# Exchanging transposed attention blocks through a scratch tensor in memory, in two halves of four heads, and letting early transposes share five PSUM banks with the mix

## The chip, the core and the metric

The kernel runs on one core of a Trainium2 chip. The metric is the device time of one execution in microseconds (us); lower is better. The core has a matrix engine (TensorE, PE in the rows; its weight loads are PEld), a vector engine (VectorE, DVE), a scalar engine (ScalarE, ACT), GpSimd (POOL) and a queue that issues transfers (SyncE, SP). Each of them runs its own instructions strictly in the order in which they are written, and waits where an instruction's inputs are not ready. Results of TensorE land in PSUM, which has eight banks of 128 x 512 float32 here; all else is held in SBUF.

## What is computed

Banded attention for 4 batches, 8 heads, 768 positions and head size 64: a position sees the first 8 keys and its last 96. Then a channel mix over the 512 channels (8 heads x 64).

```python
scores = scale * q @ k.T - slope[h] * dist          # masked outside of the band
a = softmax(scores)
x = (a @ v), heads side by side                     # [4, 768, 512]
x_prev = x moved by one position
xk = mu_k * x + (1 - mu_k) * x_prev
xr = mu_r * x + (1 - mu_r) * x_prev
kk = relu(xk @ w_k) ** 2                            # 512 -> 1024
out = sigmoid(xr @ w_r) * (kk @ w_v)                # 1024 -> 512
```

## The kernel before

The rows are cut into 24 tiles of 128 positions, six to a batch. For tile n and a pair of heads hp (0 to 3), `scores` multiplies queries with the keys of this tile and the one before (into a bank of `ps_s`), VectorE adds the bias and takes the maximum (L317), ScalarE takes the exponential (L318), and after every second pair GpSimd divides by the sums (L328). The weights of the softmax then lie with the query on the partition and must be turned, so that the key is on the partition, before `weighted` can multiply them with the values (L383, the matmuls named `av`).

Tiles 0 to 8 are turned by TensorE (`transposes`, L362) into banks of `ps_t`, and ScalarE copies them out (L363). From tile 9 on (`MOVED`), `turn` (L339, L341) has VectorE turn blocks of 32 x 32 in place into the area `turned`, and `exchange` (L349) then moves the blocks between groups of 32 partitions: 16 transfers for each tile, each from 32 partitions of `turned` to 32 partitions of `landed`, 64 KB (32 KB where the tile is the first of its batch). `turned` and `landed` each exist once.

The channel mix works on chunks of two tiles. For a chunk, `mix` makes xk and xr as pairs of a high and a low part; then TensorE makes `kp` (four banks one after the other), `z` (two) and `vps` (two), each product as three matmuls (L423 to L425), all in banks of one pool, `ps_f`. VectorE squares `kp` into `kk` (L466) and frees its bank. The first chunk works in plain float32 (L432, L453, L489), because the weights come as 64-bit words that are decoded meanwhile (`weight_begin`: L162 loads, L170 to L175 decode with three VectorE steps).

Tiles are worked in steps. In step n+1, `scores` of tile n+1 runs beside the turning of tile n; in step n+2, `weighted` of tile n is written first. Between the pairs of heads stand pieces of the mix of an earlier chunk. The order in which the program is written is not yet the order of the engines: a scheduler reorders the instructions of every engine, by its own estimate of when each is ready. So a change of a transfer or a pool can move instructions anywhere.

In the loop, the lines that matter are these:

```python
if hp == 0 and step > 1:
    for i in range(4):
        weighted(step - 2, i)
    global_v(step - 1)
if step:
    if hp < 2:
        turn(step - 1, 2 + hp)
    if hp == 1:
        exchange(step - 1)
    transposes(step - 1, hp)
```

Of the kernel before, what the change touches and what calls it, by code (L numbers as in the profile page):

```python
# [9 lines left out]
F32 = mybir.dt.float32  # L10
# [7 lines left out]
PSUM = bass.MemoryType.PSUM  # L18
# [3 lines left out]
NT = S // 128  # L22
# [3 lines left out]
MOVED = 9  # L26
# [7 lines left out]
def tile_biased_attention_channel_mix(ctx: ExitStack, tc: tile.TileContext, qT, kT, v, n_sizes, mu_kr, w_k, w_v, w_r, q_rows, k_rows, v_rows, slopes, out):  # L34
    nc = tc.nc
# [30 lines left out]
    fast = ExitStack()  # L66
    p4k = fast.enter_context(tc.tile_pool(name="p4k", bufs=3))
    kw_pool = fast.enter_context(tc.tile_pool(name="kw", bufs=2))
    q_pool = fast.enter_context(tc.tile_pool(name="qp", bufs=2))
    v_pool = fast.enter_context(tc.tile_pool(name="vp", bufs=3))  # L70
    r_pool = fast.enter_context(tc.tile_pool(name="rp", bufs=1))
    s_pool = fast.enter_context(tc.tile_pool(name="sp", bufs=3))
    x_pool = fast.enter_context(tc.tile_pool(name="xp", bufs=1))
    f_pool = fast.enter_context(tc.tile_pool(name="fp", bufs=1))
    f2_pool = fast.enter_context(tc.tile_pool(name="f2", bufs=4))
    ps_s = fast.enter_context(tc.tile_pool(name="ps_s", bufs=2, space=PSUM))
    ps_t = fast.enter_context(tc.tile_pool(name="ps_t", bufs=2, space=PSUM))
    ps_a = fast.enter_context(tc.tile_pool(name="ps_a", bufs=1, space=PSUM))
    ps_f = fast.enter_context(tc.tile_pool(name="ps_f", bufs=3, space=PSUM))


    zeros = const.tile([128, 256], BF16, name="zeros")
# [20 lines left out]
    j = flts[:, 224:352]  # L103
# [15 lines left out]
    for h in range(H):  # L119
        c = -8.0 * 2.0 ** -(h + 1)  # L120
# [14 lines left out]
    for h in range(H):  # L135
        c = -8.0 * 2.0 ** -(h + 1)
# [54 lines left out]
    def weights_go(begun):  # L191
        while w_count[0] < min(begun, len(w_steps)):
            weight_begin(w_count[0])
            w_count[0] += 1
# [6 lines left out]
    def pool_copy(dst, src):  # L201
        pool.tensor_scalar(dst, src, 1.0, 1.0, op0=ALU.mult, op1=ALU.mult)


    state = {}
    room = r_pool.tile([128, 12, 512], F32, name="room")
    turned = room[:, 4:8].rearrange("p b x -> p (b x)")
    landed = room[:, 0:4].rearrange("p a x -> p (a x)")
# [13 lines left out]
    def load_tile(n):  # L222
        b, t = divmod(n, NT)
        s = state[n] = {}
        if n < NATIVE:
            qr, kr = padded[n % 2], ring[:, n % 4]
            for o, h in sides:
                nc.sync.dma_start(qr[o : o + 64, h : h + HH], qT[n, :, h : h + HH])
                nc.sync.dma_start(kr[o : o + 64], kT[n, :, h : h + HH])
            s["qr"], s["kr"] = qr, kr  # L230
            return
        qr = p4k.tile([128, H, 128], F32, tag="t4k", name=f"qraw_{n}")
        if n == NATIVE:
            kr = kw_pool.tile([128, H, 256], F32, tag="kw", name=f"kraw_{n}")
        else:
            kr = p4k.tile([128, H, 128], F32, tag="t4k", name=f"kraw_{n}")
        for o in (0, 64):
            nc.sync.dma_start(qr[o : o + 64], qT[n])
        for o in (0, 64):
            if n == NATIVE:  # L240
                nc.sync.dma_start(kr[o : o + 64, :, 128:256], kT[n])
                if t == 1:
                    nc.sync.dma_start(kr[o : o + 64, :, 0:128], kT[n - 1])
                elif t:
                    nc.sync.dma_start(kr[o : o + 64, :, 0:32], kT[n - t, :, :, 0:32])
                    nc.sync.dma_start(kr[o : o + 64, :, 32:128], kT[n - 1, :, :, 32:128])
            else:
                nc.sync.dma_start(kr[o : o + 64], kT[n])
        s["qr"], s["kr"] = qr, kr

    def load_v(n):
        b, t = divmod(n, NT)
        va = v_pool.tile([128, DM], F32, name=f"va_{n}", tag="va")
        nc.sync.dma_start(va, v[b, t * 128 : (t + 1) * 128, :])
        state[n]["va"] = va

    def global_v(n):

        b, t = divmod(n, NT)
        if t >= 2:  # L260
            nc.sync.dma_start(state[n - 1]["va"][0:32], v[b, 0:32, :])
# [68 lines left out]
    def turn(n, hp):  # L330
        if n < MOVED:
            return
        s = state[n]
        w = 256 if n % NT else 128
        hk = w // 16
        src = room[:, 8 + hp].rearrange("p (u k) -> p u k", u=2)[:, :, 0:w]
        dst = turned[:, : 4 * hk * 32].rearrange("p (b g i) -> p g b i", b=4, g=hk)[:, hp * hk // 4 : (hp + 1) * hk // 4]
        if w == 256:
            vec.transpose(dst, src.rearrange("p u (g b j) -> p (u g) b j", b=4, j=32))  # L339
        else:  # L340
            vec.transpose(dst, src.rearrange("p u (b j) -> p u b j", b=4))  # L341

    def exchange(n):
        if n < MOVED:
            return
        m = 512 if n % NT else 256
        for b in range(4):
            for a in range(4):
                nc.sync.dma_start(landed[32 * b : 32 * b + 32, a * m : (a + 1) * m], turned[32 * a : 32 * a + 32, b * m : (b + 1) * m])  # L349

    def transposes(n, hp):
        if n >= MOVED:
            return
        s = state[n]
        nb = 2 if n % NT else 1
        pt = ps_t.tile([128, 512], F32, name=f"t_{n}_{hp}", tag="t")
        et = room[:, (4 * n + hp) % 5 if n < MOVED - 1 else hp]
        for u in range(2):
            e = s["e"].pop(2 * hp + u)
            for k in range(nb):  # L360
                c = (u * nb + k) * 128
                pe.transpose(pt[:, c : c + 128], e[:, k * 128 : (k + 1) * 128], ident)  # L362
        act.copy(et[:, : 2 * nb * 128], pt[:, : 2 * nb * 128])  # L363
        s["et", hp] = et

    def weighted(n, hp):
        t = n % NT
        s = state[n]
        if hp == 0:
            s["av"] = ps_a.tile([128, 512], F32, name=f"av_{n}", tag="av")  # L370
        blocks = [state[n - 1]["va"], s["va"]] if t else [s["va"]]
        nb = len(blocks)
        if n < MOVED:
            et = s.pop(("et", hp))
        else:
            et = landed[:, : 1024 * nb].rearrange("p (a g i) -> p g a i", a=4, i=32)
        for u in range(2):
            h = 2 * hp + u
            o = s["av"][64 * u : 64 * u + 64, hp * 128 : (hp + 1) * 128]
            for k, vt in enumerate(blocks):  # L380
                c = (u * nb + k) * 128
                g = et[:, c : c + 128] if n < MOVED else et[:, h * nb + k]
                pe.matmul(o, vt[:, h * 64 : (h + 1) * 64], g, start=k == 0, stop=k == nb - 1)  # L383
        if hp == 3:
            c, i = divmod(n, 2)
            if i == 0:
                if t == 0:
                    pool.memset(xt[:, :, 0:1], 0.0)
                else:
                    pool_copy(xt[:, :, 0:1], xt[:, :, 256:257])  # L390
            act.copy(xt[:, :, 1 + 128 * i : 129 + 128 * i], s["av"].rearrange("p (a q) -> p a q", a=4))  # L391
# [110 lines left out]
    def ffn(c):  # L502
        if c:
            xk, xr = (mix(xt[:, :, 1:257], xt[:, :, 0:256], tag, p4k, f_pool) for tag in "kr")
        else:
            xk, xr = (plain_mix(xt[:, :, 1:257], xt[:, :, 0:256], tag) for tag in "kr")
        return channel_mix(xk, xr, lambda i: out[(2 * c + i) * 128 : (2 * c + i + 1) * 128, :], f_pool, f2_pool, ps_f, c == 0, c == NCHUNK - 1)
# [20 lines left out]
    for step in range(NTILES + 1):  # L528
        if step + 1 < NTILES:
            load_tile(step + 1)  # L530
        if step < NTILES:
            load_v(step)
        for hp in range(4):
# [5 lines that stand above are left out]
                if hp < 2:  # L539
                    turn(step - 1, 2 + hp)  # L540
                if hp == 1:
                    exchange(step - 1)
                transposes(step - 1, hp)
            if step < NTILES:
                if hp > 1:
                    turn(step, hp - 2)
                scores(step, hp)
            if hp == 0:
                if step >= LAG and (step - LAG) % 2 == 0:
                    queue.append(ffn((step - LAG) // 2))  # L550
                    if len(queue) == 1 and step == LAG:
                        budget[0] = -17.5
            run_ffn(2.5)
            run_ffn(2.5)
            if hp == 1 and step + 1 < NTILES:
                split_tile(step + 1)
            slot = 4 * step + hp
            n = min(8, 2 + slot * 4 // 3) if slot < 6 else 8 + (slot - 5) * 6 // 7
            weights_go(n)
    for i in range(4):  # L560
        weighted(NTILES - 1, i)
# [171 lines left out]
```

## Time and profile before

| | |
|---|---|
| median of 3 runs | 499.7 us (495.23 to 500.42) |
| the profiled execution | 493.66 us, its span 491.9 us |
| busy in the span | PE 472.3 us (96%), DVE 372.2 us, ACT 279.9 us, POOL 261.9 us |
| granted TensorE clock | 0.999 of full speed |
| transfers | 61.55 MB, mean 125 GB/s |

The span runs from the first instruction to the last. [...] In a row of a timeline, a bracket such as [0.94 <-DMA room<-room] says how long the engine sat idle ahead of it and what ended that. `room` is the tile in which `turned` and `landed` lie, so `room<-room` is a transfer of the exchange.

### The profile page before, as it was taken

To read this page: it belongs to the slowest core of one execution; us is meant where nothing else is said; L and a number is where in the kernel's file an instruction comes from. 1 tells how busy PE (TensorE), PEld (TensorE's weight loads), DVE (VectorE), ACT (ScalarE), POOL (GpSimd) and SP (SyncE) were. 2 spreads that over 40 slices of the span, in tenths; PEclk is the share of its full clock that TensorE was granted. 3 is DMA by queue.
4 is the path that set the end of the run, shared out by engine and by line. 5 is a ranking of instruction groups with operands and counts; after the bars stand their busy time and mean duration, and the time that the engine had idled before them with its cause. 6 is when DMAs were issued, how large, how long until landed. Compare 5 with 4: busy or idle time off the path is not lost.

```text
span 491.9 us, 9755 instructions
## 1 busy us (share of the span) xinstructions
PE 472.3 (96%) x3300; PEld 404.8 (82%) x3300; DVE 372.2 (76%) x921; ACT 279.9 (57%) x654; POOL 261.9 (53%) x392
## 2 busy tenths in 40 slices
PE   8889989999999999999999999999999899999995
PEld 6568754697898898898898898898898798898985
DVE  6998978887977977877977778876977966952621
ACT  6796548254758656448558438638558448542320
POOL 6868448718657634834756724835756823703000
PEclk9999999999999999999999999999999999999999
DMA  6994690521432452483383484385364462330001
GB/s 208 304 293 136 212 229 8 130 69 45 122 93 71 107 141 69 125 210 93 112 191 95 112 211 123 103 212 127 96 169 126 125 167 65 102 97 29 26 2 49
DMA packets 32201, 61.55 MB, mean 125 GB/s; under 512 B 7056, under 2 KB 10384, under 8 KB 32144
## 3 DMA queue, kind: packets, MB, share of 16 engines
q1 hardware_dynamic: 32000, 60.85, 46.8%
q8 instruction: 28, 0.46, 0.4%
q14 instruction: 29, 0.24, 0.2%
q10 hardware_dynamic: 144, 0.00, 0.0%
HBM read 39.85 MB, written 6.29 MB: 94 GB/s over the span
## 4 chain that ended last, share of the span: by engine, by line
PE 44%; DVE 17%; DMA 11%; POOL 9%; ACT 7%; issue 5%; SPq 5%; POOLq 0%; DVEq 0%; ACTq 0%
PE vps L423 5%; PE vps L424 5%; PE vps L425 5%; POOL room L328 4%; PE kp L423 4%; PE av L383 4%; PE kp L425 4%; PE kp L424 4%; DMA kraw<-in_kT_dram 4%; DMA w<-in_w_v_dram 4%; ACT room L318 3%; SPq L349 3%; DVE room L317 3%; PE z L423 3%; PE z L424 3%
## 5 line engine op out<-in xcount | busy, mean ns | idle before, releaser
L328 POOL TENSOR_SCALAR room<-room,r 128x256 f32<-128x256 f32 (+1 forms) x192 | 122.5, 655 | 96.7 <-DVE r L325 51.6
L318 ACT ACTIVATE room<-room,nmax 128x256 f32<-128x256 f32 (+1 forms) x192 | 92.7, 485 | 73.1 <-DVE nmax L317 71.2
L423 PE MATMUL kp<-xk_hi,wk_hi 128*128 128x256 f32 x352 | 99.2, 283 | 0.0
L425 PE MATMUL kp<-xk_hi,wk_lo 128*128 128x256 f32 x352 | 98.7, 281 | 0.0
L424 PE MATMUL kp<-xk_lo,wk_hi 128*128 128x256 f32 x352 | 98.6, 280 | 0.0
L423 PE MATMUL vps<-wv_hi,kk_hi 128*128 128x512 f32 (+1 forms) x184 | 71.2, 387 | 0.0
L424 PE MATMUL vps<-wv_lo,kk_hi 128*128 128x512 f32 (+1 forms) x184 | 71.2, 387 | 0.0
L425 PE MATMUL vps<-wv_hi,kk_lo 128*128 128x512 f32 (+1 forms) x184 | 70.7, 384 | 0.0
L317 DVE CUSTOM_DVE_ANT_0 room<-s,pat 128x256 f32<-128x256 f32 (+1 forms) x192 | 68.2, 391 | 3.0 <-PE s L309 1.2
L423 PEld LDWEIGHTS kp<-xk_hi,wk_hi 128*128 128x128 f32 x352 | 66.7, 190 | 1.4 <-issue 0.8
L424 PEld LDWEIGHTS kp<-xk_lo,wk_hi 128*128 128x128 f32 x352 | 66.0, 187 | 1.0 <-issue 0.3
L425 PEld LDWEIGHTS kp<-xk_hi,wk_lo 128*128 128x128 f32 x352 | 66.0, 188 | 0.3 <-issue 0.3
L383 PE MATMUL av<-room,va 128*64 128x128 f32 x704 | 48.6, 279 | 6.0 <-DMA room<-room 2.5
L383 PEld LDWEIGHTS av<-room,va 128*64 128x64 f32 x704 | 39.5, 136 | 15.3 <-issue 9.1
L467 ACT CAST kk_hi<-kk 128x512 fp32r<-128x512 f32 x44 | 27.1, 617 | 34.0 <-DVE kk L466 34.0
L468 DVE TENSOR_TENSOR kk_lo<-kk,kk_hi 128x512 fp32r<-128x512 f32 x44 | 35.1, 797 | 15.0 <-ACT kk_hi L467 14.3
L339 DVE STREAM_TRANSPOSE room<-room 128x512 f32<-128x512 f32 x52 | 34.6, 693 | 10.7 <-POOL room L328 10.4
L400 POOL TENSOR_SCALAR mix_k<-x,mus 128x256 f32<-128x256 f32 x44 | 26.3, 616 | 28.2 <-ACT x L391 28.2
L425 PEld LDWEIGHTS vps<-wv_hi,kk_lo 128*128 128x128 f32 x184 | 34.6, 188 | 7.5 <-issue 0.2
L423 PEld LDWEIGHTS vps<-wv_hi,kk_hi 128*128 128x128 f32 x184 | 34.6, 188 | 6.8 <-issue 0.7
L424 PEld LDWEIGHTS vps<-wv_lo,kk_hi 128*128 128x128 f32 x184 | 34.5, 188 | 6.3 <-issue 0.5
L466 DVE TENSOR_TENSOR kk<-kp,kk 128x512 f32<-128x512 f32 x44 | 30.1, 683 | 10.7 <-ACT kk L460 10.5
(116 smaller groups left out, 1006.9 us busy)
## 6 DMA issues: line engine op xcount, KB each, us to landing
room<-room SPq DMA_DIRECT2D x208, 64.0 KB, 2.0
kraw<-in_kT_dram SPq DMA_DIRECT2D x36, 256.0 KB, 4.1
qraw<-in_qT_dram SPq DMA_DIRECT2D x34, 256.0 KB, 4.0
va<-in_v_dram SPq DMA_DIRECT2D x24, 256.0 KB, 3.4
out_dram<-sig SPq DMA_DIRECT2D x23, 256.0 KB, 2.2
w<-in_w_k_dram SPq DMA_DIRECT2D x8, 512.0 KB, 7.4
w<-in_w_v_dram SPq DMA_DIRECT2D x8, 512.0 KB, 6.2
w<-in_w_r_dram SPq DMA_DIRECT2D x4, 512.0 KB, 7.9
```

Of the source, the lines that this page charges most:

```text
L317: vec.tensor_tensor_reduce(out=e[:, :w], in0=o, in1=p[:, h, :], op0=ALU.add, op1=ALU.min, scale=-0.125, scalar=3.0e38, accum_out=s["nmax"] ...
L318: act.activation(e[:, :w], e[:, :w], AF.Exp, bias=s["nmax"][:, h : h + 1], scale=-1.0, accum_out=s["sum"][:, h : h + 1])
L328: pool.tensor_scalar(e[:, :w], e[:, :w], r[:, u : u + 1], 1.0, op0=ALU.mult, op1=ALU.mult)
L339: vec.transpose(dst, src.rearrange("p u (g b j) -> p (u g) b j", b=4, j=32))
L383: pe.matmul(o, vt[:, h * 64 : (h + 1) * 64], g, start=k == 0, stop=k == nb - 1)
L400: pool.tensor_scalar(tmp[:, j, :], xp[:, j, :], m1[:, j : j + 1], 1.0, op0=ALU.mult, op1=ALU.mult)
L423: pe.matmul(o, sh, mh, start=first, stop=False)
L424: pe.matmul(o, sh, ml, start=False, stop=False)
L425: pe.matmul(o, sl, mh, start=False, stop=last)
L466: vec.tensor_mul(kk, pv, kk)
L467: act.copy(kkh[:, 2 * fp : 2 * fp + 2, :], kk)
L468: vec.tensor_sub(kkl[:, 2 * fp : 2 * fp + 2, :], kk, kkh[:, 2 * fp : 2 * fp + 2, :])
```

## The change

The exchange of a tile is made in two halves, of heads 0 to 3 and of heads 4 to 7. Each half is first written as one transfer to a scratch tensor in memory (`moved`, two buffers), and then read back in four transfers, each of which fetches for 32 partitions its four blocks. The first half's exchange is written at hp 0 of the step, the second half's at hp 1. `turned` and `landed` are laid out so that each half is one piece. The pool `ps_t` with its two banks goes, and `ps_f` has five banks instead of three; the transposes of tiles 0 to 8 take theirs there.

```diff
+    d_pool = fast.enter_context(tc.tile_pool(name="dp", bufs=2, space=bass.MemoryType.DRAM))
...
-    ps_t = fast.enter_context(tc.tile_pool(name="ps_t", bufs=2, space=PSUM))
     ps_a = fast.enter_context(tc.tile_pool(name="ps_a", bufs=1, space=PSUM))
-    ps_f = fast.enter_context(tc.tile_pool(name="ps_f", bufs=3, space=PSUM))
+    ps_f = fast.enter_context(tc.tile_pool(name="ps_f", bufs=5, space=PSUM))
...
-        hk = w // 16
+        hk = w // 32
...
-        dst = turned[:, : 4 * hk * 32].rearrange("p (b g i) -> p g b i", b=4, g=hk)[:, hp * hk // 4 : (hp + 1) * hk // 4]
+        dst = turned[:, 1024 * (hp // 2) : 1024 * (hp // 2) + 128 * hk].rearrange("p (b g i) -> p g b i", b=4, g=hk)[:, hp % 2 * hk // 2 : (hp % 2 + 1) * hk // 2]
...
-    def exchange(n):
+    def exchange(n, half):
         if n < MOVED:
             return
-        m = 512 if n % NT else 256
+        m = 256 if n % NT else 128
+        s = state[n]
+        moved = d_pool.tile([128, 4 * m], F32, name=f"moved_{n}_{half}", tag="moved")
+        nc.sync.dma_start(moved, turned[:, 1024 * half : 1024 * half + 4 * m])
+        blocks = moved.rearrange("(a j) (b x) -> b j a x", a=4, b=4)
         for b in range(4):
-            for a in range(4):
-                nc.sync.dma_start(landed[32 * b : 32 * b + 32, a * m : (a + 1) * m], turned[32 * a : 32 * a + 32, b * m : (b + 1) * m])
+            nc.sync.dma_start(landed[32 * b : 32 * b + 32, 1024 * half : 1024 * half + 4 * m].rearrange("j (a x) -> j a x", a=4), blocks[b])
...
-        pt = ps_t.tile([128, 512], F32, name=f"t_{n}_{hp}", tag="t")
+        pt = ps_f.tile([128, 512], F32, name=f"t_{n}_{hp}", tag="f")
...
                 if hp == 1:
-                    exchange(step - 1)
+                    exchange(step - 1, 1)
+                if hp == 0:
+                    exchange(step - 1, 0)
```

The scheduler's order moves at three places. On TensorE, at tile 14: `av_14` are the matmuls of `weighted` for tile 14, `kp` those of the mix, `s_16_0` the first scores of tile 16. Before:

```order
L423 MATMUL kp_3308<-xk_hi_3147,wk_hi_66 128x256
L424 MATMUL kp_3308<-xk_lo_3148,wk_hi_66 128x256
L425 MATMUL kp_3308<-xk_hi_3147,wk_lo_2_783 128x256
L423 MATMUL kp_3376<-xk_hi_3147,wk_hi_66 128x256
L383 MATMUL av_14_3329<-room_194,va_13_2676 64x128
L383 MATMUL av_14_3329<-room_194,va_14_2887 64x128
```

After, from the last of `av_14` on:

```order
L386 MATMUL av_14_3304<-room_193,va_13_2663 64x128
L386 MATMUL av_14_3304<-room_193,va_14_2870 64x128
L308 MATMUL s_16_0_3331<-kw_16_3218,qh_16_3216 128x256
L309 MATMUL s_16_0_3331<-kw_16_3218,ql_16_3217 128x256
L308 MATMUL s_16_0_3331<-kw_16_3218,qh_16_3216 128x256
L309 MATMUL s_16_0_3331<-kw_16_3218,ql_16_3217 128x256
L426 MATMUL kp_3283<-xk_hi_3132,wk_hi_66 128x256
```

`av_14` has moved ahead of 17 matmuls with 256 columns: the four of `s_16_0` and 13 of `kp`, which stood before it.

On the transfer queue, the same tile: `qraw`, `kraw` and `va` are loads of queries, keys and values for later tiles, and the 16 transfers `room<-room` are the exchange of tile 14. Before:

```order
L248 DMA kraw_16_3110<-in_kT_dram 64x1024 x2
L254 DMA va_15_3115<-in_v_dram 128x512
L261 DMA va_13_2676<-in_v_dram 32x512
L349 DMA room_194<-room_194 32x512 x16
L497 DMA out_0_dram<-sig_3101 128x512
L238 DMA qraw_17_3321<-in_qT_dram 64x1024
```

After (`moved_14_0` and `moved_14_1` are the two halves):

```order
L349 DMA moved_14_0_3116<-room_193 128x1024
L352 DMA room_193<-moved_14_0_3116 32x4x256 x3
L254 DMA va_15_3094<-in_v_dram 128x512
L261 DMA va_13_2663<-in_v_dram 32x512
L352 DMA room_193<-moved_14_0_3116 32x4x256
L238 DMA qraw_17_3296<-in_qT_dram 64x1024
L349 DMA moved_14_1_3177<-room_193 128x1024
L238 DMA qraw_17_3296<-in_qT_dram 64x1024
L352 DMA room_193<-moved_14_1_3177 32x4x256 x4
L248 DMA kraw_17_3297<-in_kT_dram 64x1024 x2
```

The first half now stands ahead of the loads of values, which wait for `av_13`; behind the second turning only one write and four reads are left.

On the same queue in the first 100 us: `w64_14` to `w64_19` are loads of the weights w_v, `kraw_7` the keys of tile 7, `va_3` (32 rows) a slice that `av_4` needs, `va_5` values of tile 5. Before:

```order
L162 DMA w64_16_735<-in_w_v_dram 128x1024
L228 DMA qz_0_196<-in_qT_dram 64x512
L241 DMA kraw_7_1098<-in_kT_dram 64x8x128
L254 DMA va_5_895<-in_v_dram 128x512
L162 DMA w64_17_793<-in_w_v_dram 128x1024
L261 DMA va_3_534<-in_v_dram 32x512
L243 DMA kraw_7_1098<-in_kT_dram 64x8x128
L241 DMA kraw_7_1098<-in_kT_dram 64x8x128
L243 DMA kraw_7_1098<-in_kT_dram 64x8x128
L162 DMA w64_18_836<-in_w_v_dram 128x1024
L162 DMA w64_19_883<-in_w_v_dram 128x1024
```

After:

```order
L241 DMA kraw_7_1097<-in_kT_dram 64x8x128
L243 DMA kraw_7_1097<-in_kT_dram 64x8x128
L162 DMA w64_14_634<-in_w_v_dram 128x1024
L162 DMA w64_15_671<-in_w_v_dram 128x1024
L162 DMA w64_16_734<-in_w_v_dram 128x1024
L162 DMA w64_17_792<-in_w_v_dram 128x1024
L162 DMA w64_18_835<-in_w_v_dram 128x1024
L162 DMA w64_19_882<-in_w_v_dram 128x1024
L254 DMA va_5_894<-in_v_dram 128x512
L261 DMA va_3_533<-in_v_dram 32x512
```

All four loads of `kraw_7` now stand ahead of `w64_14`, and the slice of `va_3` behind `w64_19`. On TensorE `av_4`, of which two matmuls stood ahead of the matmuls on `z` before, now stands as a whole behind the last `vps` of the first chunk and the first `kp` of the second.

## Rows read from the trace of the kernel before

**Rows 1.** The page: the span, and TensorE's busy time.

```profile
span 491.9 us, 9755 instructions
PE 472.3 (96%) x3300; PEld 404.8 (82%) x3300; DVE 372.2 (76%) x921; ACT 279.9 (57%) x654; POOL 261.9 (53%) x392
```

**Rows 2.** TensorE's waits up to 100 us, then from 100 us on: us, times, longest.

```profile
PE av L383 <- DMA va<-in_v_dram: 2.4, 1, 2.4
PE t L362 <- POOL room L328: 2.4, 5, 0.8
...
PE av L383 <- DMA room<-room: 2.5, 2, 1.5
PE z L423 <- DVE kk L466: 1.4, 3, 0.5
```

**Rows 3.** Stretches of 20 us: busy PE, PEld, DVE, ACT, POOL; clock, DMA share, GB/s.

```profile
280.00:300.00 20.00, 18.56 (x151) 17.10 (x150) 14.39 (x33) 8.31 (x22) 7.29 (x11) 1.00 0.74 176
...
380.00:400.00 20.00, 18.49 (x145) 16.81 (x144) 15.39 (x38) 7.84 (x21) 13.01 (x20) 1.00 0.62 159
```

**Rows 4.** Timeline of TensorE at tiles 14, 15 and 20: start, us, instruction.

```profile
279.41 0.28 PE L423 MATMUL kp<-xk_hi,wk_hi 128*128 128x256 f32 x1
...
280.82 0.28 PE L423 MATMUL kp<-xk_hi,wk_hi 128*128 128x256 f32 x1
282.03 1.99 PE L383 MATMUL av<-room,va 128*64 128x128 f32 x32 [0.94 <-DMA room<-room]
...
301.32 0.39 PE L423 MATMUL vps<-wv_hi,kk_hi 128*128 128x512 f32 x1
301.55 0.39 PE L424 MATMUL vps<-wv_lo,kk_hi 128*128 128x512 f32 x1
301.87 2.02 PE L383 MATMUL av<-room,va 128*64 128x128 f32 x32
...
391.92 0.84 PE L383 MATMUL av<-room,va 128*64 128x128 f32 x11 [1.51 <-DMA room<-room]
```

**Rows 5.** Timeline of the transfer queue: exchanges of tiles 14, 15 and 20.

```profile
269.45 10.88 SPq L349 DMA_DIRECT2D room<-room  x16
...
286.90 13.04 SPq L349 DMA_DIRECT2D room<-room  x16
...
379.19 11.02 SPq L349 DMA_DIRECT2D room<-room  x16
```

**Rows 6.** Timeline of VectorE: the last turning of tile 14.

```profile
268.71 0.71 DVE L339 STREAM_TRANSPOSE room<-room 128x512 f32<-128x512 f32 x1 [0.20 <-POOL room L328]
```

**Rows 7.** Chain that ended last, by time: the last transfer of tile 12's exchange.

```profile
238.54 1.79 DMA room<-room
```

**Rows 8.** Transfers issued from 140 to 480 us: KB each, median us to landing.

```profile
room<-room SPq DMA_DIRECT2D x208, 64.0 KB, 2.0
...
out_dram<-sig SPq DMA_DIRECT2D x18, 256.0 KB, 2.2
va<-in_v_dram SPq DMA_DIRECT2D x15, 256.0 KB, 2.8
...
va<-in_v_dram SPq DMA_DIRECT2D x12, 64.0 KB, 2.6
```

**Rows 9.** First 100 us: timelines of the transfer queue, TensorE and VectorE.

```profile
61.42 0.42 SPq L261 DMA_DIRECT2D va<-in_v_dram  x1
...
68.23 0.62 PE L383 MATMUL av<-room,va 128*64 128x128 f32 x4 [2.39 <-DMA va<-in_v_dram]
...
92.56 0.38 PE L424 MATMUL kp<-xk_lo,wk_hi 128*128 128x256 f32 x1
...
49.20 0.69 DVE L173 TENSOR_SCALAR wa<-wa 128x512 int32<-128x512 int32 x1 [1.25 <-POOL wa L170]
...
52.90 1.17 DVE L174 SCALAR_TENSOR_TENSOR wa<-w,wa 128x512 int32<-128x512 int32 x1
...
89.22 1.21 DVE L403 TENSOR_TENSOR xk_lo<-mix_k,xk_hi 128x1024 fp32r<-128x1024 f32 x1
```

More of the change, by code (lines that the diff above doesn't have):

```diff
@@ L375, in weighted @@
         else:
-            et = landed[:, : 1024 * nb].rearrange("p (a g i) -> p g a i", a=4, i=32)
+            et = landed[:, 1024 * (hp // 2) : 1024 * (hp // 2) + 512 * nb].rearrange("p (a g i) -> p g a i", a=4, i=32)
         for u in range(2):
@@ L381, in weighted @@
                 c = (u * nb + k) * 128
-                g = et[:, c : c + 128] if n < MOVED else et[:, h * nb + k]
+                g = et[:, c : c + 128] if n < MOVED else et[:, h % 4 * nb + k]
                 pe.matmul(o, vt[:, h * 64 : (h + 1) * 64], g, start=k == 0, stop=k == nb - 1)
```

## The prediction, made before the run

> **What bounds the kernel now.** The page comes first: TensorE is busy 472.3 of 491.9 us, so what can be gained without taking matmuls away is 19.6 us at most [rows 1]. The waits of TensorE tell where that is. In the first 100 us it waits mostly on values, turned blocks and GpSimd; from 100 us on only two kinds of wait are worth naming: 2.5 us, in two waits, for transfers of the exchange, and 1.4 us, in three waits, where a matmul on `z` waits until VectorE's `kk` has emptied a bank [rows 2]. The stretches agree: of those after 100 us, only 280 to 300 and 380 to 400 us lose more than a microsecond (1.44 and 1.51), with the clock at 1.00 [rows 3]. So the change works on a kernel whose matmuls stand almost without a gap, and the exchange, though it keeps the queue busy for 11 to 13 us of every tile's 20 (`av` of tile 14 starts at 282.03, that of tile 15 at 301.87), costs the end only where it lands behind its consumer. Those places are tiles 14 and 20: TensorE idles 0.94 and 1.51 us ahead of `av` [rows 4].
>
> **The exchange itself.** Today's chain behind the last turning of tile 14: turned at 268.71 + 0.71 = 269.42, issues from 269.45 for 10.88 us, the last landing 1.8 us after its issue began, as at tile 12 [rows 5 to 7]; 12.5 us in all, and `av` starts at 282.03 [rows 4]. 16 issues take 0.68 us each. In the changed order one write of 512 KB and four reads of 128 KB stand behind that turning, since the first half has gone ahead. No row has a write of 512 KB; one of 256 KB lands after 2.2 us and 64 KB within SBUF after 2.0, so I take 2.8, with 2.2 and 4.4 (twice that) as ends. Reads: 64 KB of values land after 2.6 us and 256 KB after 2.8 [rows 8], so 2.7, behind three issues of 0.68. That makes 2.8 + 3 x 0.68 + 2.7 = 7.5 us, between 6.8 and 9.2; the second half would land some 5 us earlier than the whole does now.
>
> But the scheduler spends part of that. `av_14` stands 17 matmuls of 256 columns earlier than before, and such a one takes (280.82 - 279.41) / 12 = 0.12 us, so TensorE asks for the blocks 2.0 us earlier. At tile 20 it is 13 such matmuls, 1.5 us. At tile 15 it is six `z` and five `vps` at 301.55 - 301.32 = 0.23 us and four scores at 0.12, 3.0 us [rows 4]. Counted so, the 15 tiles move by 1.1 to 4.8 us. Tile 14: the wish falls on 282.03 - 0.94 - 2.0 = 279.1, the landing on 269.4 + 7.5 = 276.9; 2.2 us are left. Tile 20: 391.92 - 1.51 - 1.5 = 388.9 against 379.2 + 7.5 = 386.7, again 2.2 [rows 4, 5]. Tile 15, whose 13.04 us of issues end close ahead of `av` at 301.87, has 301.87 - 3.0 = 298.9 against 286.9 + 7.5 = 294.4 [rows 4, 5]. These are the tightest three kinds, so both waits go: **-2.5 us**. The cover runs out where the chain takes more than 7.5 + 2.2 = 9.7 us.
>
> What rides along: on the queue a tile costs 2 writes and 8 reads, 10 x 0.68 = 6.8 us of issues where 16 took 10.9, plus two waits of some 2.8 us for a write to land, each with the reads behind it on the queue. Behind the reads stand the loads for later tiles, but those wait less than now, since the queue comes free no later. The first half's reads overwrite what `av` of the tile before reads, so they wait for it; they then have a whole half step. Bytes moved rise by 14 MB (what 208 and 32 transfers move now is moved twice); the share of the transfer engines after 100 us stands at 0.62 to 0.74 in the stretches that lose time [rows 3], and nothing on TensorE waits for loads of queries or keys there, so I cost that at nothing; if a load came 1 us later, VectorE and GpSimd would hide it as now. VectorE's turnings keep their count and their size.
>
> [...] In the rows, a 256 KB write to memory lands only 0.2 us later than a 64 KB copy inside SBUF [rows 8]. [...]
>
> **The banks.** `ps_f` grows from three banks to five once tile 8 is turned. The waits of `z` for `kk` are waits for a bank, since `z` does not read `kk`; with two more the allocation is two products further ahead, and one `kp` product is 24 matmuls of 256 columns, 2.8 us, against waits of at most 0.5 us [rows 2]. **-1.4 us**; what is next, the wait of `vps` for `kk` itself, shows nowhere among TensorE's waits today. The other end is 0, if VectorE is late for other reasons: its turnings now stand singly between `kk` steps, each waiting for GpSimd.
>
> **The first 100 us.** Here the order moves, and no single view prices it. The wait of 2.39 us ahead of `av` at 68.23 is for the slice of values issued at 61.42 behind a load of weights [rows 9]; in the new order `av_4` stands behind the first chunk, and that wait goes. What is late next is the first matmul on the low part of xk, at 92.56; VectorE makes that part at 89.22 + 1.21 = 90.43, so no more than 2.1 us come back. Against it, all loads of `kraw_7` (1 MB) now stand ahead of the weights, and on VectorE the decoding of weight tile 12 stands ahead of that of tile 11. Tile 11's first step ran at 49.20 and the second step of tile 12 ended at 52.90 + 1.17 = 54.07 [rows 9], so that the chain of loads that waits for tile 11's buffer may start 4.9 us later; matmuls on `z` and scores stand between, which had been ready. Ends: -2.1 and +2.8 (4.9 less the 2.1); I take **-1.0 us**, nearer the end whose rows lie on TensorE.
>
> **The sum.** -2.5 - 1.4 - 1.0 = -4.9 us against the profiled 493.66 us, so 488.8. The median of the runs shown, 499.7, is 1.2% above the profiled execution; scaled with it, 488.8 x 499.7 / 493.66 = **494.7 us**. The forecast's own ends: all gains at their best (-6.0) 493.6, banks and early stage at their worst (-2.5 + 2.8) 500.
>
> **Rivals.** *The waits only move* (chance 0.27): VectorE stands in turnings that wait for GpSimd, `kk` or the low part of xk come late, and what the exchange gives back is lost ahead of `kp`. For it: such waits for GpSimd are in the rows of the turnings already [rows 6]; against it: 1.1 to 4.8 us of extra lead of `av`, and so of the mix that follows it. Time: within 2 us of before, 498 to 502.
>
> *The early stage gains more* (0.12): the two largest waits of the first 100 us, 2.4 us for values and 2.4 for GpSimd ahead of TensorE's turnings [rows 2], both go, since the new order asks for values and turned blocks later, and the low part of xk comes earlier by as much. That is -2.5 - 1.4 - 4.8 = -8.7, 490.9 us. Against it: VectorE's load of decoding is unchanged.
>
> *Slower, by the way through memory* (0.14): the write's landing and the four reads take as long as today's 16 copies, 12.5 us. Then `av` asks 1.1 to 4.8 us earlier for blocks that land when they land now. The move less the lead that the blocks have today is 2.0 us at tile 14, 1.5 at 20, and 2.2 at 15 (3.0 less 301.87 - 299.94 + 0.68 - 1.8, from the end of its issues). The other twelve I estimate at a third of these three's mean, 0.6 us each: 5.7 + 7.2 = 13 us, 507 in the profiled execution, 513 in the median's terms. It decides from a chain of 9.7 us on; at 10.5 us it only eats the 2.5 us.
>
> *The change does not do what it says* (in the first rival's chance): both halves go one after the other behind the last turning. Then the chain is 15 us, and the time is the last rival's and more; the order above, with `moved_14_0` ahead of the values, speaks against it.
>
> **How the numbers follow.** Forecast 0.47, the rivals 0.27, 0.12 and 0.14. A difference under 1% (5.0 us, below 494.7 or above 504.7) is about what a measurement of this kernel can't tell from none. The forecast lies on that edge, so half of its chance, 0.24, counts as faster, with the 0.12 of the early gain and a little of scatter: faster 0.39; slower 0.15 is the last rival and a tail of the first 100 us; the rest, 0.46, is within 1%. The range 489 to 505 leaves out the slow way through memory and the best of the early gains.
>
> **What would show it.** The two waits of `av` for `room<-room` are gone, and the last read of each half lands 7 to 8 us after the last turning, against 12.5; no `z` waits for `kk`; the stretches after 100 us are at 19.8 or more of 20; the transfer engines move some 75 MB; the first matmul on the low part of xk starts near 91.5. I am wrong if `av` waits for `room<-moved` at many tiles (the way through memory is slow), if TensorE waits for VectorE's xk or scores (the waits moved), or if that first matmul starts after 95.

## The result, and the profile after

The changed kernel takes 490.69 us (median of six executions, 486.83 to 493.18) against 496.77 us for the kernel before beside it: a ratio of 0.9896, with 0.9854 to 0.9938 as its 95% interval, 6.1 us less by the medians and 3.1 to 7.3 by the interval. A second comparison gave 490.08 against 495.9 us, 0.9883 (0.9841 to 0.9924). The forecast, 494.7 against 499.7, was a ratio of 0.990. In microseconds the kernel lies 4.0 us below it, 2.9 of them because the kernel before took 496.77 here and not 499.7. The profiled execution of the changed kernel lasted 493.18 us and was the slowest of its six; a second one lasted 487.29. What differs between those two lies in the first 100 us (below).

The page of the changed kernel answers to [rows 1]:

```profile
span 491.3 us, 9689 instructions
PE 473.9 (96%) x3300; PEld 408.8 (83%) x3300; DVE 382.8 (78%) x921; ACT 283.0 (58%) x656; POOL 255.8 (52%) x392
```

The view of TensorE's waits lists none from 100 us on, in either profile, where [rows 2] had 3.9 us. Up to 100 us the two largest waits of the first profile are these (us, times, longest):

```profile
PE s L305 <- DMA qz<-in_qT_dram: 5.9, 2, 3.3
PE av L386 <- ACT room L366: 1.6, 3, 0.8
```

The wait for values is gone, and one for the queries of an early tile is larger than anything in [rows 2]. The stretches of 20 us (busy PE, PEld, DVE, ACT, POOL; clock, DMA share, GB/s) that answer to [rows 3], with two of the first 100 us:

```profile
20.00:40.00 20.00, 18.20 (x136) 16.21 (x137) 17.98 (x59) 14.18 (x42) 14.63 (x21) 0.84 1.03 261
40.00:60.00 20.00, 17.40 (x106) 14.45 (x105) 14.85 (x43) 12.63 (x36) 10.33 (x18) 0.91 0.45 146
...
280.00:300.00 20.00, 20.00 (x168) 18.92 (x167) 15.88 (x38) 7.99 (x24) 11.46 (x17) 1.00 0.79 228
...
380.00:400.00 20.00, 20.00 (x149) 18.00 (x148) 18.43 (x44) 10.43 (x23) 13.99 (x22) 1.00 0.61 189
```

Both late stretches are full; every stretch from 100 us on has 19.86 or more. Timelines of VectorE, the transfer queue and TensorE show the exchange of tile 14's second half, as [rows 4 to 6] did the whole one:

```profile
272.89 0.70 DVE L339 STREAM_TRANSPOSE room<-room 128x512 f32<-128x512 f32 x1
...
273.62 0.34 SPq L349 DMA_DIRECT2D moved<-room  x1
274.02 0.47 SPq L238 DMA_DIRECT2D qraw<-in_qT_dram  x1
276.58 1.73 SPq L352 DMA_DIRECT2D room<-moved  x4
...
284.27 2.02 PE L386 MATMUL av<-room,va 128*64 128x128 f32 x32
```

The last turning ends at 273.59. The write lands at 276.52, the last read, issued at 277.88, at 280.92: a chain of 7.3 us, and `av` starts 3.4 us later without idle time. Over the 15 tiles the chain of the second half has a median of 8.4 us (7.2 to 10.4). The transfers issued from 140 to 480 us (KB each, median us to landing), beside [rows 8]:

```profile
moved<-room SPq DMA_DIRECT2D x26, 512.0 KB, 3.9
room<-moved SPq DMA_DIRECT2D x104, 128.0 KB, 3.1
...
out_dram<-sig SPq DMA_DIRECT2D x19, 256.0 KB, 3.6
va<-in_v_dram SPq DMA_DIRECT2D x15, 256.0 KB, 4.3
```

For all comparisons below TensorE's run is cut at matmul 968 (the first is 0): up to there every kernel here has issued the same matmuls, though not all in the same order, and from there on come the same 2332. **The steady part** is the time from the start of that matmul to the end of the last, read from the recorded matmuls of each profile: 332.80 and 331.95 us in two profiles of the kernel before, 327.84 in both of the changed one. So 4.1 to 5.0 us of the gain lie there. Matmul 968 starts at 153.64 and 156.30 us in the former, 158.82 and 153.05 in the latter.

Another 0.8 to 1.0 us, which the forecast did not count, lie behind the last matmul. Its row, of the kernel before and of the changed one, beside the spans of 491.9 and 491.3 us:

```profile
486.16 0.28 PE L425 MATMUL vps<-wv_hi,kk_lo 128*128 128x256 f32 x1
...
486.38 0.28 PE L428 MATMUL vps<-wv_hi,kk_lo 128*128 128x256 f32 x1
```

From its end to that of the span it is 5.46 and 5.60 us in the two profiles of the kernel before, 4.66 and 4.64 in those of the changed one, 5.45 with the banks alone and 4.69 with the halves alone. The last output lands 2.2 us behind the last matmul in all of them, so the difference lies behind that landing; its cause was not tested. The stretch ahead of matmul 968 keeps, by subtraction, between nothing and 1.2 us of the gain.

### The profile page after: what moved, and what is told of

Its sections match the earlier page's. It is cut to its first block, busy times and chain, and to the rows that moved or that the text cites. A ratio compares the mean times of both kernels' runs of the same rounds, so it can differ in the third digit from the quotient of the medians.

```text
span 491.3 us, 9689 instructions
## 1 busy us (share of the span) xinstructions
PE 473.9 (96%) x3300; PEld 408.8 (83%) x3300; DVE 382.8 (78%) x921; ACT 283.0 (58%) x656; POOL 255.8 (52%) x392
## 4 chain that ended last, share of the span: by engine, by line
PE 75%; DVE 8%; DMA 8%; POOL 3%; issue 3%; ACT 1%; SPq 0%; POOLq 0%; ACTq 0%; DVEq 0%
PE kp L426 8%; PE vps L427 8%; PE kp L428 8%; PE vps L426 8%; PE kp L427 8%; PE vps L428 8%; PE av L386 7%; DMA qz<-in_qT_dram 4%; PE z L426 4%; PE z L427 4%; PE z L428 4%; PE s L308 4%; PE s L309 3%; DMA w<-in_w_v_dram 2%; PE s L306 2%
## 5 line engine op out<-in xcount | busy, mean ns | idle before, releaser
L328 POOL TENSOR_SCALAR room<-room,r 128x256 f32<-128x256 f32 (+1 forms) x192 | 110.1, 591 | 133.0 <-DVE r L325 62.5
L339 DVE STREAM_TRANSPOSE room<-room 128x512 f32<-128x512 f32 x52 | 36.0, 702 | 18.0 <-POOL room L328 18.0
L471 DVE TENSOR_TENSOR kk_lo<-kk,kk_hi 128x512 fp32r<-128x512 f32 x44 | 33.9, 772 | 14.3 <-ACT kk_hi L470 12.8
L463 ACT ACTIVATE kk<-kp 128x512 f32<-128x512 f32 x48 | 28.2, 588 | 15.2 <-PE kp L428 13.4
```

What stands on the lines that cost most here:

```text
L328: pool.tensor_scalar(e[:, :w], e[:, :w], r[:, u : u + 1], 1.0, op0=ALU.mult, op1=ALU.mult)
L463: act.activation(kk, pv, AF.Relu)
L471: vec.tensor_sub(kkl[:, 2 * fp : 2 * fp + 2, :], kk, kkh[:, 2 * fp : 2 * fp + 2, :])
```

## The experiments

**The kernels once more.** No edit.

> The changed kernel once more, unaltered. The forecast's mechanism and every rival expect the ratio to before again, 0.990 with 0.985 to 0.994. What it tells apart is the first 100 us of the profile. If the new order of the early stage costs time of itself, TensorE again loses some 19 us in the stretches from 0 to 60 us (20.0 - 13.3, 18.2 and 17.4 summed to 11.1 after the start-up part), with waits of about 3 us for qz and a clock of 0.84 to 0.91 between 20 and 60 us, and the span stays near 491. If that was an accident of the one profiled execution, the clock there is back near 0.99, the waits for qz are at most 1 us each, and the span is near 485 to 488, which is 4 to 6 us below the 491.9 of before and so the size of the forecast's sum.

Measured: 0.9883 as above, a span of 485.5 us. The wait for `qz` was 1.2 us in place of 5.9, the clock from 20 to 40 us 0.92, and the first matmul on the low part of xk started at 92.24, not 97.97. So most of the early loss of the first profile belongs to that execution and not to the kernel, though the clock and the wait did not come back as far as expected.

> The kernel before once more, unaltered: a ratio of 1.000. What it tells is how far one profiled execution of it stands for others. If the waits that the forecast counted belong to the kernel, its steady part, from matmul 968 to the end, is again near 332.8 us (332 to 335) with the av waits for room<-room and the z or kp waits for VectorE near the same places, where the changed kernel has 327.84 in both of its profiles. If they were accidents of one execution, the steady part comes near 328 to 331 us, and the gain of the changed kernel would have another cause.

Measured: 495.59 us, 0.9967 (0.9921 to 1.0014), steady part 331.95. The waits belong to the kernel. From 100 us on:

```profile
PE av L383 <- DMA room<-room: 2.6, 2, 1.4
PE z L423 <- DVE kk L466: 1.0, 2, 0.8
```

**The banks alone.** In the kernel before, only:

```
-    ps_t = ...(name="ps_t", bufs=2, space=PSUM)
-    ps_f = ...(name="ps_f", bufs=3, space=PSUM)
+    ps_f = ...(name="ps_f", bufs=5, space=PSUM)
...
-        pt = ps_t.tile(...)
+        pt = ps_f.tile(...)
```

> The kernel before with the five shared banks and nothing else: the exchange stays at 16 copies of 64 KB. Its order up to the first exchange is that of the changed kernel. The forecast prices this at -1.4 (no z waits for kk) - 1.0 (first 100 us) = -2.4 us, a ratio of 0.995 (0.991 to 1.003): the two av waits for room<-room near 282 and 392 us stay, 2.5 us or somewhat more in all, since av and the mix run no later than before. The rival, that the banks are the whole gain, expects 0.990 as in the changed kernel; the other rival, that waits only move, expects 1.000.

Measured: 495.45 us, 0.9989 (0.9954 to 1.0024); steady part 331.32 us. From 100 us on TensorE waits here:

```profile
PE av L382 <- DMA room<-room: 2.5, 3, 1.4
PE kp L423 <- DVE xk_lo L402: 0.6, 1, 0.6
```

The `z` waits are gone and the `av` waits stay, as forecast; a new wait for the low part of xk takes some of it back. In the steady part the banks are worth 0.6 to 1.5 us, too little for the timing to tell from nothing.

**The halves alone.** The changed kernel with `ps_t` of two and `ps_f` of three banks again.

> The exchange in two halves through memory, with the banks as before (two for the turnings of TensorE, three for the mix). Its order up to the first exchange is that of the kernel before. The forecast prices this at -2.5 us, a ratio of 0.995 (0.990 to 1.000): no av waits for room<-moved, the three waits of z for kk, 1.4 us, stay. The rival, that the exchange was hidden well enough and gives nothing, expects 1.000; a slow way through memory would show as av waits and a ratio above 1.000.

Measured: 491.21 us, 0.9894 (0.9848 to 0.994); steady part 327.84 us, that of the changed kernel to the hundredth. TensorE waits nowhere after 100 us, not for blocks and, with three banks, not on `z` either. So the halved exchange brings the whole steady gain, and the banks add nothing to it. That speaks against the forecast's split of the sum. From matmul 968 on TensorE's order here is that of the changed kernel too, so the earlier `av` came with the halves; what the new order is worth by itself was not tested.

**One piece through memory.** The exchange at `hp == 1` as before, but as

```
+        nc.sync.dma_start(moved, turned[:, : 4 * m])
+        for b in range(4):
+            nc.sync.dma_start(landed[32 * b : 32 * b + 32, : 4 * m]..., blocks[b])
```

with `m = 512`, five banks.

> The changed kernel with the exchange in one piece: one write of 1 MB and four reads of 256 KB behind the last turning, in place of two halves. TensorE's order is that of the changed kernel, instruction for instruction. The chain behind the last turning, by the rows of the changed kernel (512 KB written in 3.9 us, 128 KB read in 3.1, three issues of 0.45 us): twice the bytes add 1 to 4 us to the write and up to 1 us to the reads, so 9.5 to 13 us where a half takes 8.3. The forecast, with its limit of 9.7 us, expects av to wait for the blocks at several tiles, 0.5 to 2 us each: a ratio of 0.993 to 1.005. The rival, that few issues give the gain and the halves nothing, expects 0.990, no waits, and all stretches after 100 us at 19.9 or more.

Measured: 500.95 us, 1.01 (1.0058 to 1.0141), slower than the kernel before and beyond the range expected; steady part 335.90. TensorE's waits from 100 us on, its transfers, and the worst place, tile 19:

```profile
PE av L386 <- DMA room<-moved: 3.7, 3, 2.2
PE av L386 <- ACT kk_hi L470: 1.4, 2, 0.8
PE av L386 <- ACT room L318: 1.1, 1, 1.1
...
moved<-room SPq DMA_DIRECT2D x13, 1024.0 KB, 4.2
room<-moved SPq DMA_DIRECT2D x52, 256.0 KB, 5.2
...
377.00 2.51 PE L386 MATMUL av<-room,va 128*64 128x128 f32 x32 [2.23 <-DMA room<-moved]
```

The last two lines of waits are also the exchange: at each of the six places the last read landed some 0.1 us before `av` started, and the engine named had long been done. The chain has a median of 11.7 us (8.0 to 13.9). In this order of TensorE, which asks for the blocks early, a way through memory with five issues is therefore no gain by itself; the halves are what takes the chain off the path.

**Halves without memory.** Each half by 16 direct copies of 32 KB.

```
+        for b in range(4):
+            for a in range(4):
+                o = 1024 * half
+                nc.sync.dma_start(landed[32 * b : 32 * b + 32, o + a * m : o + (a + 1) * m],
+                                  turned[32 * a : 32 * a + 32, o + b * m : o + (b + 1) * m])
```

> The changed kernel with its two halves, but without memory: each half goes by 16 direct copies of 32 KB, so 32 issues for a tile. If halving alone brings the gain, the ratio to before is 0.990. If the few issues are what makes halves possible, the queue is the bound: 32 issues of 0.5 to 0.68 us and six loads take 19 to 25 us of a tile that lasts 18, so 1 to 7 us more for each of 15 tiles, a ratio of 1.03 to 1.2 with waits of av for room<-room at nearly every tile.

Measured: 608.56 us, 1.2287 (1.2215 to 1.2359). One row of the transfer queue's timeline:

```profile
355.67 20.96 SPq L350 DMA_DIRECT2D room<-room  x31
```

31 issues take 20.96 us, 0.68 each, longer than the 18 us from `av` to `av` in the changed kernel: the queue is the bound, and the loss is a little beyond the range expected. TensorE waits 30.2 us for blocks and 52.5 for `xk_hi`, which is made from late `av`. Halves and the few issues need each other.

**A longer chain, the same order.** Another copy within memory between write and reads:

```
+        again = d_pool.tile([128, 4 * m], F32, name=f"again_{n}_{half}", tag="again")
+        nc.sync.dma_start(again, moved)
+        blocks = again.rearrange("(a j) (b x) -> b j a x", a=4, b=4)
```

> The changed kernel, with every half written to memory, copied once more within memory, and only then read back. The orders of TensorE and VectorE are those of the changed kernel, instruction for instruction; only the chain from a turning to its landed blocks is longer, by one transfer of 512 KB. By the rows of the changed kernel (512 KB in 3.9 us) and more, if a copy within memory is slower, 4 to 8 us: from 8.3 to 12 to 16 us. The second half lands 2.5 to 4.4 us before its first matmul there, and the forecast has its limit at 9.7 us: it expects av to wait for the blocks at most of the 15 tiles, 1 to 5 us each, and a ratio to before of 1.01 to 1.10. The rival, that the exchange was hidden anyway and its length decides nothing, expects 0.989 as in the changed kernel.

Measured: 552.42 us, 1.1157 (1.1096 to 1.1218); steady part 385.26 us. From 100 us on:

```profile
PE av L388 <- DMA room<-again: 39.1, 13, 5.9
```

The chain has a median of 18 us, more than the copy's 3.9 us added: the queue stands at each of the two landings (one half's write is issued at 267.20 us, its copy at 272.29, its reads from 276.27 on), and the write of a half starts only when the reads of the half before are out (the next one at 278.09, behind reads whose issues end at 278.00). The loss is beyond the range expected.

**A little longer.** Each read split into two of 16 partitions.

```
+            for j in (0, 16):
+                nc.sync.dma_start(landed[32 * b + j : 32 * b + j + 16, ...], blocks[b, j : j + 16])
```

> The changed kernel with every read of a half split into two reads of 64 KB over 16 partitions, so eight issues in place of four: four more issues of 0.35 to 0.48 us, 1.4 to 1.9 us on a chain of 8.3. TensorE's order is unchanged. It tests the point from which the chain decides. The forecast put that at 9.7 us behind the last turning: then a chain of 9.7 to 10.3 begins to show, with av waits of up to 0.6 us at the tightest tiles and a ratio 0.000 to 0.003 above that of the changed kernel. By the landings of the changed kernel, 2.5 to 4.4 us ahead of their first matmul, the point lies near 11 us: no wait of av for room<-moved, and a steady part of 327.8 us as there.

Measured: 495.54 us, 0.9995 (0.9968 to 1.0023): the whole gain is gone. Steady part 334.07. The chain of the second half has a median of 10.1 us, and `av` waits at tiles 11 and 15, where it took 12.4 and 13.4. Tile 15, and the stretch with its wait:

```profile
289.41 0.71 DVE L339 STREAM_TRANSPOSE room<-room 128x512 f32<-128x512 f32 x1 [0.20 <-POOL room L328]
...
290.10 3.07 SPq L353 DMA_DIRECT2D room<-moved  x5
293.27 0.37 SPq L349 DMA_DIRECT2D moved<-room  x1
298.06 3.58 SPq L353 DMA_DIRECT2D room<-moved  x8
...
300.19 1.14 PE L387 MATMUL av<-room,va 128*64 128x128 f32 x16
303.55 1.27 PE L387 MATMUL av<-room,va 128*64 128x128 f32 x16 [2.22 <-DMA room<-moved]
...
300.00:320.00 20.00, 17.78 (x102) 14.58 (x101) 18.34 (x44) 14.62 (x29) 11.25 (x20) 0.91 0.63 189
```

The turning ends at 290.12, but the write waits until 293.27: the first half's reads are still on the queue. The first 16 matmuls of `av` run on the first half, the second 16 wait. Chain less wait gives the point from which it decides: 13.4 - 2.2 = 11.2 us here, 12.4 - 2.0 = 10.4 at tile 11; at tile 17 a chain of 12.5 cost nothing. In the one-piece kernel the same difference is 9.9 to 11.5 us at its six places. Both expectations were wrong on the loss: the point is near 11 us here, as the second had it, but at these two tiles the chain came to 12 to 13 us, where both took some 10, because the write stood behind the first half's reads. The two waits make 4.2 of the 6.2 us lost. Behind the second the granted clock fell: 0.61 and 0.54 in the two stretches of 2 us from 304 to 308 us, and 1.00 in the stretches ahead of them and behind; behind the 1.99 us wait at tile 11 it stayed at 1.00.

**Where the z waits came from.** In the kernel before, the loads of queries and keys from ScalarE's queue:

```
-            nc.sync.dma_start(qr[o : o + 64], qT[n])
+            nc.scalar.dma_start(qr[o : o + 64], qT[n])
```

and the same for `kr`: queries from tile 7 on, keys from tile 8.

> The kernel before (16 direct copies, three banks), with the loads of queries and keys of tiles 8 to 23 issued from ScalarE's queue in place of SP's, so that they no longer stand behind the 16 issues of the exchange. It tests where the three waits of z for kk came from. One theory: these loads land late, GpSimd waits 5.7 us for them near 282 us, VectorE's ql and kw behind it stand ahead of kk, and kk comes late; then those z waits and GpSimd's waits for qraw and kraw go although the banks stay three, and the steady part (from matmul 968 to the end) falls from 332.8 us by 1.5 or more, to 331 or less; av may still wait for room<-room. The rival, that three banks are too few, expects z waits for kk of 1.4 us in all to stay and a steady part of 332 or more. Ratio to before: 0.994 to 0.998 by the first, 1.000 by the second; ScalarE pays four issues of some 0.5 us a tile in both.

Measured: 522.44 us, 1.0532 (1.048 to 1.0584); steady part 359.15. No wait of `z` for `kk` and none of `av` for blocks, but TensorE waits 12.2 us for `xk_lo` and 6.3 for `xk_hi`, and the scheduler had reordered TensorE. With TensorE that late, the missing `z` waits say nothing. Inconclusive.

So the other way round: in the kernel with halves and three banks, and in the changed one, the loads are held back.

```
-        if step + 1 < NTILES:
+        if step + 1 < NTILES and step <= MOVED:
             load_tile(step + 1)
...
+            if hp == 1 and MOVED < step < NTILES - 1:
+                with tc.issue_after(reads[-1]):
+                    load_tile(step + 1)
```

> The halves through memory with the old three banks, in which the loads of queries and keys of tiles 11 to 23 are held back until the last read of the exchange of the tile two before has been issued. TensorE's order is that of the kernel with halves and three banks, instruction for instruction. If the z waits for kk of the kernel before came from loads that stand behind the exchange on the queue (its loads of tile 16 were issued from 281.05 us, one microsecond before av of tile 14, and landed at 285 to 290; here they are issued some 5 us ahead of that av, in the halves-only kernel from 270 us), part of them returns: GpSimd waits for qraw or kraw, VectorE's ql and kw come late, and z or kp waits for VectorE, 0.3 to 1.5 us in all; the steady part from matmul 968 to the end goes from 327.8 to 328 to 330 us. If the loads' place has no part in it, the steady part stays at 327.8 and TensorE waits nowhere.

> The same held-back loads in the changed kernel, so with five banks. If late loads bring z waits back and the banks cover them, this has fewer waits than the kernel with three banks and a steady part of 327.8 to 328.5 us; if the banks do nothing there, both lose the same; if the loads' place has no part in it, both stay at 327.8.

Measured: 532.28 us, 1.073 (1.0682 to 1.0777), and 530.85 us, 1.0698 (1.0647 to 1.0749); steady parts 369.96 and 368.95. The losses expected in the steady part, 2.2 us at most, were far too small. TensorE's one kind of wait from 100 us on, with three and with five banks, and a place in the former (queue, GpSimd, VectorE, TensorE):

```profile
PE s L309 <- DVE kw L284: 29.5, 12, 4.7
```

```profile
PE s L308 <- DVE kw L283: 30.0, 12, 3.9
```

```profile
286.75 1.73 SPq L355 DMA_DIRECT2D room<-moved  x4
288.58 1.11 SPq L239 DMA_DIRECT2D qraw<-in_qT_dram  x2
...
294.91 1.04 POOL L203 TENSOR_SCALAR qh<-qraw 128x1024 fp32r<-128x1024 f32 x1 [1.39 <-DMA qraw<-in_qT_dram]
296.32 1.79 POOL L203 TENSOR_SCALAR kw<-kraw 128x1024 fp32r<-128x1024 f32 x1 [0.37 <-DMA kraw<-in_kT_dram]
...
298.15 1.41 DVE L284 TENSOR_TENSOR kw<-kraw,kw 64x1024 fp32r<-64x1024 f32 x1 [0.25 <-POOL kw L203]
...
299.61 0.38 PE L309 MATMUL s<-kw,qh 128*128 128x256 f32 x1 [3.30 <-DVE kw L284]
```

Loads behind the exchange close a ring: exchange, loads, GpSimd's and VectorE's split, scores, turning, next exchange. The banks cover nothing of it. The place of these loads on the queue is a price of its own; that it was the source of the `z` waits is not shown by this, since the wait that it brought is on scores.

**The early queries.** The changed kernel with a third buffer for padded queries, in unused space of the one that holds `firsts`, and loads two tiles ahead.

```
-    qr, kr = padded[n % 2], ring[:, n % 4]
+    qr, kr = padded[n % 3], ring[:, n % 4]
...
+        if 1 < step + 2 < NATIVE:
+            load_tile(step + 2)
```

> The changed kernel with a third buffer for the padded queries of tiles 0 to 6, in space that a half-empty buffer had, so that tile n + 2 instead of n + 1 is loaded in a step: the queries and keys of tile 2 go ahead of the first four loads of weights. If the accident of the profiled executions (queries of tile 2 landing at 17.9 to 21.5 us behind 2 MB of weights, TensorE idle for 1.0 to 4.4 us, then a clock of 0.83 to 0.92 from 20 to 40 us) is what the first 100 us lose and what scatters the times between 487 and 494 us, this wait is gone, the clock from 20 to 40 us is at 0.95 or more, and the ratio is 0.980 to 0.986 with a scatter of 3 us or less. The rival, that the weights, the decoding on VectorE or the values come later by as much, expects 0.989 and the same scatter.

Measured: 489.53 us, 0.989 (0.9838 to 0.9942), within 489.19 to 493.62: the rival. No wait for `qz` is left, yet the first 100 us lose as much:

```profile
PE t L366 <- POOL room L329: 2.4, 1, 2.4
PE t L366 <- DVE kk L466: 1.8, 1, 1.8
PE s L306 <- DVE nmax L318: 1.6, 2, 1.4
```

The clock from 20 to 40 us is 0.83. The wait for `qz` stood for a stage in which several inputs come late together. No version here beats the changed kernel: this one and the halves alone equal it.

## Why the prediction was right, point by point

**The exchange, -2.5 us: right.** Both waits of `av` went, with and without the banks. The chain was mis-sized a little: the write took 3.9 us where 2.8 was taken (inside the ends), the issues 0.35 to 0.48 us where 0.68 was, the reads 3.1 where 2.7 was; 8.4 us in place of 7.5, inside 6.8 to 9.2. The first tile's and last tile's second halves, 10.0 and 10.4, passed 9.7 and cost nothing. Of the old chain one row was misread: [rows 7] is the 13th of tile 12's 16 transfers, and its 1.79 us a piece of the chain and not its way to landing; at tile 14 the last transfer is issued at 279.74 and lands at 281.79 us, 2.05 us, so nothing in the sum hangs on it.

**What rides along, nothing: wrong as a reason.** The loads of queries were costed at nothing because no wait on TensorE named them. But timelines of the queue, GpSimd and VectorE in the kernel before show what stands ahead of the `z` wait that ends at 294.02 us:

```profile
282.24 0.50 SPq L238 DMA_DIRECT2D qraw<-in_qT_dram  x1
...
287.51 1.04 POOL L202 TENSOR_SCALAR qh<-qraw 128x1024 fp32r<-128x1024 f32 x1 [5.70 <-DMA qraw<-in_qT_dram]
...
288.59 1.22 DVE L282 TENSOR_TENSOR ql<-qraw,qh 128x1024 fp32r<-128x1024 f32 x1 [2.81 <-POOL qh L202]
...
291.33 1.22 DVE L283 TENSOR_TENSOR kw<-kraw,kw 64x1024 fp32r<-64x1024 f32 x1
...
293.27 0.69 DVE L466 TENSOR_TENSOR kk<-kp,kk 128x512 f32<-128x512 f32 x1
...
294.02 0.50 PE L423 MATMUL z<-wr_hi,xr_hi 128*128 128x512 f32 x1 [0.50 <-DVE kk L466]
```

The loads stand behind the 16 issues, land at 287 us, GpSimd waits 5.70 us, VectorE 2.81, and `kk` is queued behind. The same stands ahead of the other two `z` waits, where GpSimd waits 3.73 and 4.39 us, and of both in the second profile (5.70 and 3.91). With the halves the same copy of queries runs without a wait, although with three banks:

```profile
282.75 1.06 POOL L203 TENSOR_SCALAR qh<-qraw 128x1024 fp32r<-128x1024 f32 x1
...
287.37 1.23 DVE L284 TENSOR_TENSOR kw<-kraw,kw 64x1024 fp32r<-64x1024 f32 x1
```

**The banks, -1.4 us: right size alone, counted twice.** Alone they are worth 0.6 to 1.5 us of the steady part; beside the halves, 0.00. The step that failed is that the wait was put down to a shortage of banks alone, so that the two terms were added. They overlap: the exchange takes the same wait away by another way. GpSimd's waits for queries, before and with the banks alone:

```profile
POOL qh L202 <- DMA qraw<-in_qT_dram: 21.8, 5, 5.7
...
POOL qh L201 <- DMA qraw<-in_qT_dram: 20.1, 5, 4.9
```

With five banks the loads are as late as before and `z` does not wait; with the halves and three banks GpSimd has no such wait, and `z` does not wait either. So by these rows the wait took both, late loads and three banks; a run that makes the loads late without more harm, and so shows it, is missing.

The sum came out near the measured ratio partly by luck. The steady gain of the exchange alone, 4.1 to 5.0 us, holds both terms: the view lists 3.9 and 3.6 us of waits in the two profiles of the kernel before. It counts each wait from the end of the row ahead, and such a row lasts 0.28 us where the pace from start to start is 0.12 [rows 4]; 0.16 us more for each of five and four waits makes 4.7 and 4.2 of the 5.0 and 4.1 us. And the -1.0 for the early stage met a gain of about that size behind the last matmul, which no term had.

**The first 100 us, -1.0 us: not to be told.** Up to matmul 514 all of these kernels have again issued the same ones. Matmul 514 started between 93.96 and 99.84 us in eight profiles with the new early order, mean 96.2, and between 94.07 and 100.44 in five with the old one, mean 96.9. The difference of 0.8 us has the forecast's sign and an eighth of the scatter. "After 95" for the first matmul on the low part of xk was a bad sign to name: it came true in one profile of the changed kernel (97.97) and in one of the kernel before (96.32), so it tells of the execution and not of the change.

**The rivals.** "The waits only move" happened nowhere: the steady part of 327.84 us has no wait left. "Slower, by the way through memory" is a true mechanism in the wrong kernel: with one piece it came, at a chain of 11.7 us and 1.01. The point from which it decides, 9.7 us, is 9.9 to 11.5 at the places that showed it, but none of these was tile 14 or 20, from which the forecast had worked it out: in the one-piece kernel a chain of 13.9 us cost nothing at tile 20. The changed kernel stands close to it: of its 15 tiles the tightest is tile 19, whose last read lands 0.7 us, in the second profile 1.4, ahead of the first matmul that needs it; the 2.5 to 4.4 us that two of the expectations took for all tiles does not hold there. The scaling to the median of 499.7 cost nothing in the ratio; in the later comparisons that kernel's median was 495 to 497.

## What to carry to other kernels

A wait that names an engine is followed back to what that engine waited for before its price is given to an edit; here a wait for a bank began on the transfer queue, and two terms of a sum were one. On a queue that runs in order, count what stands behind every transfer that waits: few issues, a chain cut in halves, and the loads of later tiles free to slip in between were all needed. Before a gain of 1% is explained, take a second profile of each kernel: the part that repeats (here to the hundredth in the changed kernel, within 0.9 us in the one before) carries the reason, and the part that scatters by 6 us carries none.

## What the hardware showed that was not expected

Between the changed kernel and the one-piece one, doubling a write to memory from 512 KB to 1 MB moved its median landing from 3.9 to 4.2 us, while doubling a read from 128 to 256 KB moved it from 3.1 to 5.2. In the changed kernel other transfers landed later too: 256 KB of output 3.6 us where it was 2.2, values 4.3 (3.5 in the second profile) where it was 2.8 [rows 8]; in the one-piece kernel the two are 4.1 and 2.8. The granted clock was lower behind some of TensorE's idle times: 0.91 in the stretch with the 2.22 us wait of the eight reads, 0.84 from 20 to 40 us behind the wait of 3.3 us that ends at 20.5 us in the changed kernel (0.50 from 20 to 26 us, and 1.00 from 28 to 40), and 0.83 there in the kernel with early queries, where TensorE was busy for 16.03 of the 20 us; the single 1.51 us of [rows 4] left its stretch at 1.00 [rows 3].
